# Moving three kinds of side work one place later in a fused attention and feed-forward kernel on Trainium2

## The chip, the cores and the metric

The kernel runs on one core of one Trainium2 chip. Its engines work at the same time, each through its own queue in order: TensorE (PE in the profile; PEld is its weight load), VectorE (DVE), ScalarE (ACT), GpSimd (POOL), and SyncE (SP), which issues most DMAs. They wait for each other through semaphores. The metric is the device time of one execution in microseconds (us), less is better.

## The reference

Three stages in float32, on 2304 tokens (4 batches of 576):

```python
scores = where(0 <= i - j < 64, q @ k.T / 8, -1e9)      # 8 heads of 64, causal window of 64
x = (softmax(scores) @ v)                               # laid out as [2304, 512]
x2 = ((x @ w1) * (x @ w2)) @ w3 @ w_out                 # 512 -> 1024 -> 1024 -> 512
h = x2 @ w_in                                           # 512 -> 2048
out = (h * sigmoid(h)) @ w_out2                         # 2048 -> 512
```

The weights come in as float64 and are turned into float32 on the chip.

## The kernel before

Every matrix product of float32 quality is made of three passes: an operand is split into a high part (a cast, mostly on ACT) and a low part (the difference, mostly on POOL), and high times high, high times low and low times high are summed in PSUM.

The tokens are cut into 6 blocks of 384 (`NB`). `phase_a(blk)` computes the first feed-forward stage of a block in 24 units: units 0 to 15 compute `ab` (one accumulator each; an even unit is x @ w1, copied by ACT at L582, the odd one behind it x @ w2, multiplied with it by DVE at L584 and split into `p` or `q`), units 16 to 23 compute `x2` in halves (four accumulators, copied by ACT at L561). The input of a block is `xa` and `xb`, the splits of `xr`: two of four 128-row parts, c = 0, 1, in `xa`, c = 2, 3 in `xb`. Unit 0 of a block uses c = 0, 1, 2 and then 3; for each c its three passes read high, low, high of the input.

Between the units the attention of the next block is worked in. It consists of groups (two heads, 128 queries), 12 to a block, and `half(h)` issues them in halves, two units to a group:

- an even half (even unit) issues for group g the scores (L317, L321, then DVE L327), for g - 2 the product with the values (`values`, L394 and L395), for g - 1 the transposes `t` of the normalised probabilities `sm` (L360) and their copies to `pt` (ACT L370, L372, DVE L373, L375), then the exponentials of g (ACT L338);
- an odd half issues `normalise(g)` (DVE L346, L348 and the multiply L350), the output sum of g - 2 (`total`: ACT copies L402, L403, DVE adds L404, L405, POOL add L406 into `xr`), the split of the next keys (ACT L292 `qkhi`, POOL L296 `klo`, DVE L299) and of the next values (`vhl`, ACT and POOL), and the next loads.

For the last group of a block the output sum is already issued at the end of the even half, in unit 22, ahead of the normalise in unit 23, and the last part of the next block's input (c = 3) is split right behind it, also in unit 22 (`split_x`, o == 3, f == 0). The other three parts are split in units 17, 19 and 21. Only groups from 17 on (`PLAIN`) have an output sum of this kind.

In blocks 1 to 4 the weight `w_in` is converted as well, in 16 chunks of 6 units (`Stored.pieces`): scale and rest on ACT, fraction and two halves of the sign on DVE, and with the second half of the sign the integer sum of 128x512 words on POOL (L181), in place 8 of a chunk, that is in units 2, 8, 14 and 20 of a block; the store is issued two places later. `squeeze(u)` issues the piece that is due at place u.

The last stage runs over 3 super blocks of 8 slices, `step(s, k)` with k = 0 to 6: seven products (L781) into two accumulators `hx` and `hy` in the place of eight, read by ACT and DVE between them, and the products with `w_out2` (L835). The operands of the products of the next super block are sums of parts of x2 (`x_sum`), made in the last slice: `X_AT` says at which (slice, k).

The order on each engine is the order in which this code issues the instructions (a manual schedule); only semaphores can hold an instruction back.

Of the kernel before, what the change touches and what calls it, by code (L numbers as in the profile page):

```python
# [14 lines left out]
ALU = mybir.AluOpType  # L15
# [8 lines left out]
NBLK = T // NB  # L24
NU = T // 128
NPAIR = H // 2
# [16 lines left out]
def tile_window_attention_ffn(ctx, tc, qkv, vp, mask, ident, w1, w2, w3t, w_out, w_in, w_out2, out):  # L43
# [7 lines left out]
    nc = tc.nc  # L51
# [7 lines left out]
    def f32(ap):  # L59
        return ap.bitcast(F32)  # L60
# [92 lines left out]
    class Stored(Chunk):  # L153
# [3 lines left out]
        def pieces(self):  # L157


            def scale():  # L160
                w = self.words.rearrange("p (n two) -> p n two", two=2)
                self.high = w[:, :, 1]
                self.b = slot("cv_b", "cv_b", [512], I32, bufs=CVB)
                nc.scalar.activation(out=f32(self.b), in_=f32(self.high), func=AF.Copy, scale=2.0**-112)

            def rest():
                low = self.words.rearrange("p (n two) -> p n two", two=2)[:, :, 0]
                self.r = slot("cv_r", "cv_r", [512], I32, bufs=CVR)
                nc.scalar.activation(out=self.r, in_=low.bitcast(U32), func=AF.Copy, scale=2.0**-29)

            def fraction():
                nc.vector.tensor_scalar(out=self.b, in0=self.b, scalar1=3, scalar2=None, op0=ALU.logical_shift_left)

            def sign(i):
                n = slice(i * 256, i * 256 + 256)
                nc.vector.scalar_tensor_tensor(
                    out=self.b[:, n], in0=self.high[:, n], scalar=-0x80000000, in1=self.b[:, n],
                    op0=ALU.bitwise_and, op1=ALU.bitwise_or,
                )
                if i:  # L180
                    nc.gpsimd.tensor_tensor(out=self.b, in0=self.b, in1=self.r, op=ALU.add)  # L181

            def store():
                nc.sync.dma_start(out=self.out, in_=f32(self.b))

            return [self.load, scale, rest, fraction, lambda: sign(0), lambda: sign(1), store]

    weights = {}
    line = []
    between, unit_of = {}, [0]  # L190

    def squeeze(u):
        if u in between:
            between.pop(u)()
    done = {"load": 0, "step": 0}

    def loads_to(n):
# [33 lines left out]


    NG = NU * NPAIR
    LAST_HALF = 2 * NG + 3
    qk_raw, v_raw, qk_st, v_st, s_st, p_st = {}, {}, {}, {}, {}, {}
    pt = {}

# [15 lines left out]
    def plain(g):  # L253


        return g < PLAIN
# [153 lines left out]
    def half(h):  # L410

        g, odd = divmod(h, 2)
        if not odd:
            if g < NG:
                scores(g)
            squeeze(unit_of[0])
            if 2 <= g <= NG + 1:
                sums.append(values(g - 2))  # L420
                if plain(g - 2):
                    sums.pop()()
            if 1 <= g <= NG:
                split_t(g - 1, transposes(g - 1))
            if g < NG:
                exps(g)
            if sums and (g - 2) % (3 * NPAIR) == 3 * NPAIR - 1:
                sums.pop()()
        else:
            if g < NG:  # L430
                normalise(g)
            if sums:
                sums.pop()()
            prep_qk(g + 2)
            if g < NG:
                prep_v(g)

            for x in range(g + 2, g + 5):
                if plain(x) and x > g + 2:
                    break  # L440
                load_qk(x)
            for x in range(g + 1, g + 4):
                if g < (x - 1 if plain(x - 3) else x - 3):
                    break
                load_v(x)

    halves, sums = [0], []

    def halves_to(n):
        while halves[0] < min(n, LAST_HALF):  # L450
            half(halves[0])
            halves[0] += 1

    def split_x(blk, c):
        if c == 0:
            xhl[blk] = [slot(f"{t}{blk}", t, [2, 2, NB], F32R) for t in ("xa", "xb")]
        x = xhl[blk][c // 2][:, c % 2]
        split(x[:, 0], x[:, 1], xr[:, c], "act", "pool")
# [93 lines left out]
    def phase_a(blk, hooks):  # L552
        x = xhl[blk]
        p = [slot(f"p{blk}", "p", [5, 2, NB], F32R), slot(f"q{blk}", "q", [3, 2, NB], F32R)]
        p = [p[f // 5][:, f % 5] for f in range(8)]
        a_sb = None

        def finish_x2(o, acc):
            squeeze(unit_of[0] - 1)
            x2 = slot(f"x2s{blk}_{o}", "st", [NB], bufs=4)  # L560
            nc.scalar.copy(out=x2, in_=acc)  # L561
            nc.scalar.dma_start(out=x2d[o, :, blk * NB : (blk + 1) * NB], in_=x2)

        def unit(n):
            halves_to(W_HALVES + 24 * blk + n + 1)
            hooks(n)

        for s in range(16):
            f, m = divmod(s, 2)
            unit(s)  # L570
            fs = slice((f % 4) * 128, (f % 4 + 1) * 128)
            acc = accumulator(f"ab{blk}_{s}", [128, NB])
            for k in range(4):
                w = weights["12", (2 * m + f // 4) * 4 + k]
                for n, (l, r) in enumerate(PASSES):
                    nc.tensor.matmul(  # L576
                        acc, lhsT=w[:, l, fs], rhs=x[k // 2][:, k % 2, r, :],
                        start=(k == 0 and n == 0), stop=(k == 3 and n == 2),
                    )
            if m == 0:  # L580
                a_sb = slot(f"a{blk}_{f}", "st", [2, NB], bufs=4)
                nc.scalar.copy(out=a_sb[:, 0], in_=acc)  # L582
            else:
                nc.vector.tensor_tensor(out=a_sb[:, 1], in0=acc, in1=a_sb[:, 0], op=ALU.mult)  # L584
                squeeze(unit_of[0] - 1)
                split(p[f][:, 0], p[f][:, 1], a_sb[:, 1], "act", "pool")
        kept = []
        for o in range(4):
            acc = accumulator(f"x2_{blk}_{o}", [128, NB])
            for f in range(8):  # L590
                if f % 4 == 0:
                    unit(16 + 2 * o + f // 4)
                    if blk + 1 < NBLK and o == 3 and f == 0:
                        split_x(blk + 1, 3)
                    if blk + 1 < NBLK and o < 3 and f == 4:
                        split_x(blk + 1, o)
                for n, (l, r) in enumerate(((0, 0), (1, 0), (0, 1))):
                    if o == 0 and f == 7 and n == 2:
                        continue
                    nc.tensor.matmul(  # L600
                        acc, lhsT=wp[f][:, l, o * 128 : (o + 1) * 128], rhs=p[f][:, r, :],
                        start=(f == 0 and n == 0), stop=(f == 7 and n == 2),
                    )
                if kept and f == 1:
                    first = kept.pop()
                    nc.tensor.matmul(
                        first, lhsT=wp[7][:, 0, 0:128], rhs=p[7][:, 1, :], start=False, stop=True
                    )
                    finish_x2(0, first)
            if o == 0:  # L610
                kept.append(acc)
            else:
                finish_x2(o, acc)
# [11 lines left out]
    with tc.manual_schedule():  # L625
# [5 lines left out]
        for i in range(16):  # L631
            qq, k = divmod(i, 4)
            cols = slice(qq * 512, (qq + 1) * 512)
            c = Stored(None, w_in[k * 128 : (k + 1) * 128, cols], xe[:, i % 2 * 1024 : i % 2 * 1024 + 1024], w_in32[k, :, cols])
            load, scale, rest, fraction, sign0, sign1, store = c.pieces()
            at = 6 * i
            chunks.append((load, store))
            between[at + 1], between[at + 3] = scale, rest
            between[at + 4], between[at + 6], between[at + 8] = fraction, sign0, sign1

        def drop(n):
            u = unit_of[0]
# [12 lines left out]
        for blk in range(1, NBLK - 1):  # L655
            phase_a(blk, drop)
        for u in sorted(between):
            between.pop(u)()
        chunks[15][1]()
        late.close()  # L660
        converting.update(z=lambda: ps.tile([128, 512], I32, name="cv_z", tag="ps3"), banks=3)
# [203 lines left out]
        def x_op(j, i):  # L865
            b11, b12, b21, b22 = x_sources()
            src = (b11, b11, b21, b12, b21, tmp["t1"], b22)[i]
            n = OPS * j + i
            x_tile(n)
            x_high(n, src)  # L870
            later.append(lambda: x_low(n, src))

        def x_sum(i):
# [13 lines left out]
        X_AT = {  # L887
            (5, 0): lambda j: x_raw(j), (5, 3): lambda j: x_sum(0), (6, 2): lambda j: x_sum(2),
            (6, 4): lambda j: x_op(j, 0), (6, 6): lambda j: x_sum(1), (7, 1): lambda j: x_op(j, 1),
            (7, 2): lambda j: x_op(j, 2), (7, 4): lambda j: x_sum(3), (7, 5): lambda j: x_op(j, 3),  # L890
            (8, 0): lambda j: x_op(j, 4), (8, 2): lambda j: x_op(j, 5), (8, 3): lambda j: x_op(j, 6),
        }

# [177 lines left out]
```

## Time and profile before

| what | value |
|---|---|
| median of 3 runs | 844.87 us (844.01 to 845.13) |
| the profiled execution | 844.38 us, of which the span from first to last instruction is 842.6 us |
| PE busy | 824.5 us, 98% of the span |
| DVE, ACT, POOL busy | 614.4, 560.8, 530.6 us |
| granted TensorE clock | 1.00 in the whole span |
| attention beside `phase_a`, blocks 1 to 4 | 159.6 to 412.5 us of the span |
| last block and last stage | 412.5 to 842 us |

PE busy is a sum over stages, and its matmuls are pipelined, so that small gaps between them show better in the starting times of a timeline than in the share. The chain that ended last (68% PE, 7% ACT, 6% POOL, 4% issue, 3% DVE) passes through PE for most of the span, and through ACT, DVE and POOL in parts of blocks 1 to 4.

### The profile page before, as it was taken

The page shows a single profiled execution, that of the slowest core. Times are in us where ns is not written, and L with a number is a line of the kernel's source. Part 1 is how long each engine was busy: PE and PEld are TensorE (multiplying, and loading weights), DVE is VectorE, ACT ScalarE, POOL GpSimd, SP SyncE. Part 2 cuts the span into 40 slices and gives each one's busy share as a digit, 9 for nine tenths or more (in the row PEclk, how much of TensorE's full clock was granted, in tenths as well). Part 3 has the DMA queues.
Part 4 walks back from the last instruction along what each step waited for, and adds up shares of the span by engine and source line. Part 5 has one row for each costly group of instructions (what it writes and reads, how often), then busy time and mean ns, then how long its engine had stood idle before and what let it go on. Part 6 is the DMA issues. An engine that isn't in the chain of part 4 may idle for free.

```text
span 842.6 us, 14171 instructions
## 1 busy us (share of the span) xinstructions
PE 824.5 (98%) x4410; PEld 744.9 (88%) x4410; DVE 614.4 (73%) x1420; ACT 560.8 (67%) x1389; POOL 530.6 (63%) x588
## 2 busy tenths in 40 slices
PE   5999999999999999999999999999999999999998
PEld 2555799999999999999999998888898888888986
DVE  5879877688888888888368698998644568644544
ACT  5889778898898899898556566546543446443433
POOL 5669676677677677677465577876455457454441
PEclk9999999999999999999999999999999999999999
DMA  8999334434544554543443522301301201201001
GB/s 299 315 309 289 106 96 125 145 118 142 167 157 144 170 157 145 169 152 107 134 154 114 200 75 75 125 26 51 101 25 45 106 26 63 88 25 51 1 1 75
DMA packets 57130, 102.66 MB, mean 122 GB/s; under 512 B 5472, under 2 KB 34912, under 8 KB 57056
## 3 DMA queue, kind: packets, MB, share of 16 engines
q1 hardware_dynamic: 53600, 97.05, 35.7%
q10 hardware_dynamic: 3456, 4.72, 1.5%
q8 instruction: 35, 0.57, 0.3%
q14 instruction: 39, 0.32, 0.1%
HBM read 88.11 MB, written 13.63 MB: 121 GB/s over the span
## 4 chain that ended last, share of the span: by engine, by line
PE 68%; ACT 7%; POOL 6%; issue 4%; DVE 3%; ACTq 0%; POOLq 0%; DVEq 0%
PE o L835 22%; PE ab L576 16%; PE hy L781 11%; PE hx L781 9%; PE x L600 6%; POOL klo L296 2%; ACT sm L338 1%; PE t L360 1%; POOL xr L406 1%; POOL vhl L84 1%; ACT qkhi L292 1%; PE o L394 1%; POOL p L84 1%; PE s L317 1%; POOL q L84 1%
## 5 line engine op out<-in xcount | busy, mean ns | idle before, releaser
L835 PE MATMUL o<-hl,gp 128*128 128x512 f32 x504 | 133.3, 394 | 0.0
L576 PE MATMUL ab<-xa,hl 128*128 128x384 f32 x576 | 119.0, 341 | 0.0
L781 PE MATMUL hy<-xop,j 128*128 128x384 f32 x576 | 116.0, 335 | 0.5 <-DVE tmp L675 0.5
L576 PE MATMUL ab<-xb,hl 128*128 128x384 f32 x576 | 115.4, 334 | 0.0
L84 POOL TENSOR_TENSOR gp<-tmp,gp 128x384 fp32r<-128x384 f32 x56 | 63.5, 1134 | 79.5 <-ACT gp L81 77.9
L781 PEld LDWEIGHTS hy<-xop,j 128*128 128x128 f32 x576 | 102.7, 188 | 9.8 <-DVE tmp L675 1.6
L835 PEld LDWEIGHTS o<-hl,gp 128*128 128x128 f32 x504 | 93.1, 188 | 13.1
L576 PEld LDWEIGHTS ab<-xb,hl 128*128 128x128 f32 x576 | 101.3, 188 | 0.0
L797 ACT ACTIVATE tmp<-hx 128x384 f32<-128x384 f32 x48 | 23.6, 492 | 114.0 <-DVE hx L675 69.2
L576 PEld LDWEIGHTS ab<-xa,hl 128*128 128x128 f32 x576 | 99.1, 188 | 0.0
L675 DVE TENSOR_TENSOR tmp<-hy,tmp 128x384 f32<-128x384 f32 x96 | 53.2, 554 | 56.9 <-PE hy L781 52.0
L781 PE MATMUL hx<-xop,j 128*128 128x384 f32 x432 | 86.6, 335 | 0.0
L835 PE MATMUL o<-hl,gq 128*128 128x512 f32 x324 | 85.9, 393 | 0.0
L84 POOL TENSOR_TENSOR gq<-tmp,gq 128x384 fp32r<-128x384 f32 x36 | 40.0, 1111 | 72.6 <-ACT gq L81 72.6
L781 PEld LDWEIGHTS hx<-xop,j 128*128 128x128 f32 x432 | 76.8, 188 | 4.2
L406 POOL TENSOR_TENSOR xr<-ot 128x128 f32<-128x128 f32 x55 | 32.3, 587 | 73.9 <-DVE ot L405 65.8
L296 POOL TENSOR_TENSOR klo<-qk,qkhi 64x192 fp32r<-64x192 f32 x110 | 68.0, 618 | 7.6 <-ACT qkhi L292 2.7
L835 PEld LDWEIGHTS o<-hl,gq 128*128 128x128 f32 x324 | 60.3, 188 | 11.2
L600 PE MATMUL x<-p,wp 128*128 128x384 f32 x360 | 69.6, 339 | 0.0
L338 ACT ACTIVATE sm<-sm,nm 128x192 f32<-128x192 f32 x144 | 64.5, 450 | 3.8 <-DVE nm L327 2.4
L600 PEld LDWEIGHTS x<-p,wp 128*128 128x128 f32 x360 | 61.8, 188 | 0.0
L137 POOL TENSOR_TENSOR cv_b<-cv_b,cv_r 128x512 int32<-128x512 int32 x32 | 48.6, 1520 | 18.7 <-DVE cv_b L133 9.4
(138 smaller groups left out, 1887.4 us busy)
## 6 DMA issues: line engine op xcount, KB each, us to landing
qk<-in_qkv SPq DMA_DIRECT2D x55, 384.0 KB, 3.2
words<-in_w_out SPq DMA_DIRECT2D x24, 512.0 KB, 5.4
r<-w_in SPq DMA_DIRECT2D x22, 512.0 KB, 3.4
words<-in_w3t SPq DMA_DIRECT2D x16, 512.0 KB, 6.6
words<-in_w SPq DMA_DIRECT2D x16, 512.0 KB, 6.6
xe<-in_w_in SPq DMA_DIRECT2D x16, 512.0 KB, 4.6
v<-in_qkv SPq DMA_DIRECT2D x55, 96.0 KB, 2.7
x2d<-x2s ACTq DMA_DIRECT2D x24, 192.0 KB, 1.9
```

What stands on the lines that cost most here:

```text
L84: (nc.vector if eng_lo == "dve" else nc.gpsimd).tensor_tensor(out=lo, in0=src, in1=f32(hi), op=ALU.subtract)
L137: nc.gpsimd.tensor_tensor(out=x, in0=b, in1=self.r, op=ALU.add)
L292: nc.scalar.copy(out=hi, in_=t)
L296: nc.gpsimd.tensor_tensor(out=k_lo[g % 2][hs, h * 192 : h * 192 + 192], in0=t[hs, n], in1=f32(hi[hs, n]), op=ALU.subtract)
L338: nc.scalar.activation(out=x, in_=x, func=AF.Exp, scale=-1.0, bias=nm[:, h : h + 1], accum_out=sums_of[g % 2][:, h, 0:1])
L406: nc.gpsimd.tensor_tensor(out=xr[:, c, r : r + 128], in0=t[:, 0:128], in1=t[:, 128:256], op=ALU.add)
L576: nc.tensor.matmul(acc, lhsT=w[:, l, fs], rhs=x[k // 2][:, k % 2, r, :], start=(k == 0 and n == 0), stop=(k == 3 and n == 2),)
L600: nc.tensor.matmul(acc, lhsT=wp[f][:, l, o * 128 : (o + 1) * 128], rhs=p[f][:, r, :], start=(f == 0 and n == 0), stop=(f == 7 and n == 2),)
L675: eng.tensor_tensor(out=out, in0=a, in1=b, op=op)
L781: nc.tensor.matmul(bank[name], lhsT=w[:, l, at + kt], rhs=x[:, kt, r, :], start=(fresh and kt == 0 and n == 0), stop=(kt == 1 and n == 2), ...
L797: nc.scalar.activation(out=sg, in_=src, func=AF.Sigmoid)
L835: nc.tensor.matmul(oacc[t], lhsT=g[:, l, cols], rhs=weights["out", 2 * p + i][:, r, :], start=(p == 0 and i == 0 and n == 0), stop=(p == P ...
```

## The change

Three edits:

1. The output sum of a block's last group is issued in the odd half of unit 23, behind `normalise` and so like that of every other group; the last part of the next block's input (c = 3) is split in unit 23, behind the split of the next keys and values, in place of unit 22. `LAST_HALF` grows by one so that the last group of all still gets its sum.
2. The integer sum of a `w_in` chunk on POOL becomes a piece of its own, one place later: units 3, 9, 15 and 21 of a block. Where two pieces are due at one place, both are issued, the older chunk's first.
3. In the last stage the slice sum `x_sum(3)` (DVE, 128x768) is issued at (7, 6), behind the low part of the fourth operand, instead of at (7, 4).

```diff
-                if i:
-                    nc.gpsimd.tensor_tensor(out=self.b, in0=self.b, in1=self.r, op=ALU.add)
+
+            def whole():
+                nc.gpsimd.tensor_tensor(out=self.b, in0=self.b, in1=self.r, op=ALU.add)
...
-            return [self.load, scale, rest, fraction, lambda: sign(0), lambda: sign(1), store]
+            return [self.load, scale, rest, fraction, lambda: sign(0), lambda: sign(1), whole, store]
...
     def squeeze(u):
-        if u in between:
-            between.pop(u)()
+        for f in between.pop(u, ()):
+            f()
...
-    LAST_HALF = 2 * NG + 3
+    LAST_HALF = 2 * NG + 4
...
             if g < NG:
                 exps(g)
-            if sums and (g - 2) % (3 * NPAIR) == 3 * NPAIR - 1:
-                sums.pop()()
...
                     unit(16 + 2 * o + f // 4)
-                    if blk + 1 < NBLK and o == 3 and f == 0:
-                        split_x(blk + 1, 3)
-                    if blk + 1 < NBLK and o < 3 and f == 4:
+                    if blk + 1 < NBLK and f == 4:
                         split_x(blk + 1, o)
...
-            load, scale, rest, fraction, sign0, sign1, store = c.pieces()
-            at = 6 * i
+            load, *pieces, store = c.pieces()
             chunks.append((load, store))
-            between[at + 1], between[at + 3] = scale, rest
-            between[at + 4], between[at + 6], between[at + 8] = fraction, sign0, sign1
+            for at, f in zip((1, 3, 4, 6, 8, 9), pieces):
+                between.setdefault(6 * i + at, []).append(f)
...
-            (7, 2): lambda j: x_op(j, 2), (7, 4): lambda j: x_sum(3), (7, 5): lambda j: x_op(j, 3),
+            (7, 2): lambda j: x_op(j, 2), (7, 5): lambda j: x_op(j, 3), (7, 6): lambda j: x_sum(3),
```

Where POOL goes from block 3 to block 4, its row of instructions before is this (cv_b is the integer sum of w_in, xr the add of an output sum, klo and vhl the low parts of the next keys and values, xb4 the low parts of block 4's input, first c = 2, then c = 3):

```order
L181 TENSOR_TENSOR cv_b_4338<-cv_b_4338,cv_r_4419 128x512
L406 TENSOR_TENSOR xr_88<-ot58_4623 128x128
L296 TENSOR_TENSOR klo0_75<-qk62_4479,qkhi62_4629 64x192 x2
L84 TENSOR_TENSOR vhl60_4634<-v60_4403,vhl60_4634 128x3x64
L84 TENSOR_TENSOR xb4_4484<-xr_88,xb4_4484 128x384
L406 TENSOR_TENSOR xr_88<-ot59_4686 128x128
L84 TENSOR_TENSOR xb4_4484<-xr_88,xb4_4484 128x384
L296 TENSOR_TENSOR klo1_76<-qk63_4557,qkhi63_4710 64x192 x2
L84 TENSOR_TENSOR vhl61_4715<-v61_4481,vhl61_4715 128x3x64
```

and in the changed kernel, at the same place:

```order
L407 TENSOR_TENSOR xr_88<-ot58_4622 128x128
L297 TENSOR_TENSOR klo0_75<-qk62_4479,qkhi62_4628 64x192 x2
L84 TENSOR_TENSOR vhl60_4633<-v60_4402,vhl60_4633 128x3x64
L84 TENSOR_TENSOR xb4_4484<-xr_88,xb4_4484 128x384
L182 TENSOR_TENSOR cv_b_4338<-cv_b_4338,cv_r_4419 128x512
L407 TENSOR_TENSOR xr_88<-ot59_4702 128x128
L297 TENSOR_TENSOR klo1_76<-qk63_4557,qkhi63_4708 64x192 x2
L84 TENSOR_TENSOR vhl61_4713<-v61_4481,vhl61_4713 128x3x64
L84 TENSOR_TENSOR xb4_4484<-xr_88,xb4_4484 128x384
```

The integer sum went from ahead of the first four rows to behind them, and the low part of c = 3 from ahead of klo and vhl to behind them.

At the same place on DVE (rs and sm are the normalise of group 61, ot59 the output sum of the block's last group) the row is, before:

```order
L375 TENSOR_TENSOR pt0_975<-t60_4674,pt0_975 64x64 x2
L404 TENSOR_TENSOR ot59_4686<-o59_4670,ot59_4686 64x256
L405 TENSOR_TENSOR ot59_4686<-o59_4670,ot59_4686 64x256
L346 TENSOR_REDUCE rs61_4666<-es1_83 128x2
L348 RECIPROCAL rs61_4666<-rs61_4666 128x2
L350 TENSOR_TENSOR sm1_74<-sm1_74,rs61_4666 128x384
```

and in the changed kernel:

```order
L376 TENSOR_TENSOR pt0_975<-t60_4674,pt0_975 64x64 x2
L347 TENSOR_REDUCE rs61_4666<-es1_83 128x2
L349 RECIPROCAL rs61_4666<-rs61_4666 128x2
L351 TENSOR_TENSOR sm1_74<-sm1_74,rs61_4666 128x384
L405 TENSOR_TENSOR ot59_4702<-o59_4670,ot59_4702 64x256
L406 TENSOR_TENSOR ot59_4702<-o59_4670,ot59_4702 64x256
```

The two adds of the output sum changed places with the normalise. TensorE's own order is the same in both kernels.

## Rows read from the trace of the kernel before

**Rows 1.** Waits of TensorE: engine, line, releaser: us in total, times, longest us

```profile
PE t L360 <- ACT xb L81: 1.3, 5, 0.3
PE hy L781 <- DVE tmp L675: 0.5, 1, 0.5
```

**Rows 2.** Stages: us, busy PE, PEld, DVE, ACT, POOL, PE clock, DMA share, GB/s

```profile
287.40:351.40 64.00, 63.52 (x400) 63.10 (x398) 54.82 (x176) 56.41 (x165) 46.81 (x65) 1.00 0.51 157
...
412.50:475.00 62.50, 62.50 (x359) 61.97 (x358) 41.88 (x53) 35.65 (x68) 38.37 (x34) 1.00 0.48 163
```

**Rows 3.** Timeline, TensorE, blocks 3 to 4: start us, us, engine, line, instruction

```profile
344.92 0.28 PE L395 MATMUL o<-pt,vhl 128*128 128x256 f32 x1
345.41 0.52 PE L360 MATMUL t<-id_sb,sm 128*128 128x128 f32 x3 [0.22 <-ACT xb L81]
...
351.11 0.52 PE L360 MATMUL t<-id_sb,sm 128*128 128x128 f32 x3 [0.26 <-ACT xb L81]
...
352.53 1.20 PE L576 MATMUL ab<-xb,hl 128*128 128x384 f32 x6
...
356.28 0.28 PE L395 MATMUL o<-pt,vhl 128*128 128x256 f32 x1
356.40 0.49 PE L360 MATMUL t<-id_sb,sm 128*128 128x128 f32 x3
```

**Rows 4.** Timeline, VectorE: the normalise multiplies of units 17, 21 and 23

```profile
333.63 0.56 DVE L350 TENSOR_TENSOR sm<-sm,rs 128x384 f32<-128x384 f32 x1
...
343.61 1.65 DVE L350 TENSOR_TENSOR sm<-sm,rs 128x384 f32<-128x384 f32 x1
...
350.41 0.56 DVE L350 TENSOR_TENSOR sm<-sm,rs 128x384 f32<-128x384 f32 x1
```

**Rows 5.** Timeline, GpSimd: units 17, 18 and the end of block 3

```profile
335.15 0.58 POOL L406 TENSOR_TENSOR xr<-ot 128x128 f32<-128x128 f32 x1 [1.44 <-DVE ot L405]
...
337.67 1.01 POOL L84 TENSOR_TENSOR xa<-xr,xa 128x384 fp32r<-128x384 f32 x1
...
343.56 1.29 POOL L181 TENSOR_TENSOR cv_b<-cv_b,cv_r 128x512 int32<-128x512 int32 x1
...
351.15 1.01 POOL L84 TENSOR_TENSOR xb<-xr,xb 128x384 fp32r<-128x384 f32 x1 [0.62 <-ACT xb L81]
352.12 1.46 POOL L296 TENSOR_TENSOR klo<-qk,qkhi 64x192 fp32r<-64x192 f32 x2
```

**Rows 6.** Timeline, ScalarE: ends of exponentials in units 16 and 22, and block 4's beginning

```profile
333.02 0.18 ACT L338 ACTIVATION_READ_ACCUMULATOR sm<-sm,nm 128x1 f32 x1
...
348.20 0.19 ACT L338 ACTIVATION_READ_ACCUMULATOR sm<-sm,nm 128x1 f32 x1
...
350.56 0.51 ACT L81 CAST xb<-xr 128x384 fp32r<-128x384 f32 x1 [1.53 <-POOL xr L406]
...
354.57 0.48 ACT L582 COPY a<-ab 128x384 f32<-128x384 f32 x1
```

**Rows 7.** Timeline, ScalarE and TensorE, from block 0 to block 1

```profile
156.23 0.19 ACT L338 ACTIVATION_READ_ACCUMULATOR sm<-sm,nm 128x1 f32 x1
...
160.82 1.20 PE L576 MATMUL ab<-xb,hl 128*128 128x384 f32 x6
```

**Rows 8.** Timeline, VectorE, then TensorE, slices 7 and 8 of the last stage

```profile
577.17 0.94 DVE L675 TENSOR_TENSOR xe<-xe,xra 128x768 f32<-128x768 f32 x1
...
578.51 0.54 DVE L675 TENSOR_TENSOR tmp<-hy,tmp 128x384 f32<-128x384 f32 x1
...
583.99 0.56 DVE L675 TENSOR_TENSOR tmp<-hy,tmp 128x384 f32<-128x384 f32 x1 [0.42 <-PE hy L781]
...
577.07 1.55 PE L835 MATMUL o<-hl,gp 128*128 128x512 f32 x6
579.11 1.31 PE L781 MATMUL hy<-xop,j 128*128 128x384 f32 x6 [0.48 <-DVE tmp L675]
...
587.55 1.21 PE L781 MATMUL hy<-xop,j 128*128 128x384 f32 x6
```

More of the change, by code (lines that the diff above doesn't have):

```diff
@@ L657, in tile_window_attention_ffn @@
         for u in sorted(between):
-            between.pop(u)()
+            squeeze(u)
         chunks[15][1]()
```

## The prediction

> **What bounds the kernel now.** I read the waits of TensorE first [rows 1]: in the attention stage its transposes `t` wait five times, 1.3 us together, and in the last stage one product `hy` waits 0.48. Then the stages [rows 2]: block 3 has 63.52 us of TensorE work in 64.00, and after the attention, from 412.5 on, 62.50 in 62.50. So TensorE sets the pace, nothing behind block 4 can take up a delay, and what it gains or loses between units 16 and 1 of a block stays in the time unless it is given back inside blocks 1 to 4.
>
> The waits are larger than the view lists. Normally `t` starts 0.12 us after the second product with the values (356.28, 356.40); at 345.41 it starts 0.49 after it, 0.37 late, of which 0.22 is flagged [rows 3]. Adding that 0.15 to each of the five, they cost 1.3 + 5 x 0.15 = 2.05 us. They stand at unit 0 of blocks 2, 3 and 4 and at unit 22 of blocks 2 and 3. (Some smaller, unflagged ones I leave out.) The profile names ACT xb as the releaser, but `t` needs the normalise: in both cases in [rows 3] `t` starts 0.14 to 0.15 after the end of L350 (343.61 + 1.65 = 345.26; 350.41 + 0.56 = 350.97) [rows 4].
>
> At unit 22 the reason is a collision. L350 took 1.65 us in place of 0.56: the integer sum on POOL had begun at 343.56, 0.05 ahead of it, ended at 344.85, and L350 ended 0.41 later [rows 4, 5]. The Trainium skill (SBUF — State Buffer, Who interferes with whom) says that a VectorE instruction with two SBUF inputs and a GpSimd instruction that reads SBUF contend for a shared pair of ports, that whoever issues first has it for the whole instruction, and that issue order decides who blocks. This pair of rows agrees. At unit 0 the reason is the order: normalise stands behind the adds of the output sum.
>
> **Edit 2, the integer sum.** It removes the 0.37 at unit 22. At its new place in unit 21 it follows the low part of c = 2 on POOL; what that does to unit 23 is under edit 1. In units 3, 9 and 15 it goes ahead of the low part of `p` or `q`, so that the next normalise meets an instruction of 1.29 us instead of one of 1.01 [rows 5]: at most 0.3 each, and at unit 17, where slack is least, in three blocks 0.9 in all. I take 0, since TensorE, made late by edit 1, has the slack; 0.9 goes into the range. The integer sum itself has no reader near; the store that waits for it on SP stands one place later still, with loads behind it that are not due for a unit.
>
> **Edit 1, the output sum and c = 3.** Step by step from block 3 to block 4.
> - The exponentials of unit 22 end at 348.39 [rows 6]. In unit 17 the multiply starts 0.43 after them (333.20, 333.63) [rows 4, 6], so in unit 23 it is ready at 348.82, not at 350.41.
> - POOL: in unit 17 the add `xr` starts 1.52 after that multiply starts (335.15) and the low part behind `klo` and `vhl` ends 3.53 after that (338.68) [rows 5]. In unit 21, with its multiply no longer held, `xr` starts at 345.13, the low part of c = 2 ends at 348.66, and the integer sum follows at once, to 349.9. It is ahead of the multiply by some 0.2 us. So the collision moves with it: L350 ends at 349.9 + 0.41 = 350.3, and `t` can go at 350.45.
> - TensorE, without the 0.37 and its own 0.41 (0.26 + 0.15), would be at `t` at 351.11 - 0.78 = 350.33. This wait is practically gone.
> - But the input c = 3 is now last. Adds and `xr` follow L350's end by 0.96 (334.19 to 335.15): `xr` at 351.3. Then POOL does `klo`, `vhl` and only then the low part: 3.53 later, 354.85. Before it stood ahead of `klo` and ended at 351.15 + 1.01 = 352.16 [rows 5].
> - TensorE needs this low part in unit 0: of the six matmuls at 352.53 [rows 3] the first three are c = 2, the fifth reads the low part of c = 3, some 0.7 in: 353.2. Before, the margin was 1.0 us. After, it comes there at 353.2 - 0.8 = 352.4, or up to 0.4 later where it has been late against ScalarE; I take 352.6. **A new wait of 354.85 - 352.6 = 2.2 us.** Bounds: 1.65 if TensorE has gained nothing by then (353.2), 2.5 if it has all of it.
>
> Does it come back? ScalarE's copy of unit 0 starts at 354.57 [rows 6]; with the last two matmuls of the accumulator ending near 355.4 it slides by 0.8. ScalarE works in order, and all that the next boundary rests on (`pt`, exponentials, output sums, casts) is behind that copy. So TensorE and the side work slide together, and the next boundary pays again. The gain on ScalarE, which stood 1.53 us at 350.56 waiting for `xr` [rows 6], isn't one either: with `xr` now ending near 351.9, that cast waits longer, behind `qkhi` and `vhl`.
>
> Three boundaries (to blocks 2, 3, 4) pay 2.2 each: 6.6. From block 0 to 1 there is no `w_in` work yet, so no collision: exponentials end at 156.42 [rows 7], multiply 156.85 to 157.41, `xr` 158.37, low part 161.9; TensorE needs it at 160.82 + 0.7 = 161.5 [rows 7]: 0.4 us. From block 4 to 5 no normalise is left and POOL holds no `klo` and `vhl`: 0.
>
> **Edit 3, the slice sum.** The product `hy` at 579.11 waited for the DVE add of 578.51 to 579.05, behind the slice sum of 0.94 us at 577.17 [rows 8]. Without it the add ends near 578.15, before TensorE wants to start: the flagged 0.48 and the 0.15 that is not flagged are saved, 0.65. At the new place the sum delays the add of 583.99 by 0.94, or by 1.7 if POOL is reading then; it would end by 586.3, and the next `hy` product starts at 587.55 [rows 8]: cost 0. The same sum one super block later makes no wait before, and saves none.
>
> **Sum:** -2.05 - 0.65 + 0.4 + 6.6 = +4.3 us on the profiled execution's 844.38: 848.7. That run lies 0.49 below the median of 844.87; the small waits left out, about as large in sum, pull the other way, so I leave it at **848.7 us**.
>
> **Rivals.**
> 1. *Normalise first.* The multiply is issued before the integer sum in unit 23; the margin is 0.2 us on times pieced together from unit 17. Then L350 runs 348.82 to 349.38, the integer sum after it to about 350.7, still ahead of `xr` in POOL's queue; `xr` at 350.7 instead of 351.3, the low part 0.6 to 0.7 earlier, three times: 848.7 - 2.1 = 846.6. The skill's rule on issue order, named above, leads to this if DVE is first and to the forecast if POOL is.
> 2. *The low part is in time (not slower).* If POOL finished it by 352.6, 2.2 us before my time, the gains stand alone: 844.38 - 2.7 = 841.7. For it: 1.0 us of margin before, and a normalise ready 1.6 earlier. Against it: `klo` and `vhl` ahead of it in POOL's order, 3.53 from `xr` to its end. Halfway, if each boundary cost only what the first does: 844.38 - 2.7 + 4 x 0.4 = 843.3.
> 3. *Clock.* After a wait of 2 us the granted clock falls from 2.4 to 1.2 GHz and the next two units' 4.2 us take twice as long: three times 4.2 more, 861. Against it: 1.00 in both stages of [rows 2] with their waits, though none of those is as long.
>
> **Chances.** Forecast 0.70, rival 1 0.13, rival 2 0.05 and its halfway case 0.07, rival 3 0.02, other slower ends 0.03. A measurement of this kernel can tell about 0.2%, 1.7 us: 843.2 to 846.6 counts as no change. Slower: 0.70, half of rival 1, rival 3, the rest: 0.81. Same: half of rival 1 and most of the halfway case: 0.13. Faster: 0.06. The range takes in rival 1 with a little more (845.8) and, above, waits of 2.5 each and the 0.9 of edit 2 (850.5).
>
> **What would show it.** Right: a wait of TensorE at L575 for POOL `xb` at unit 0 of blocks 1 to 4, about 0.4 and then three near 2.2; the low part of c = 3 behind `vhl`; L351 of unit 23 some 1.5 us long; no flagged wait of `t` at unit 22; no wait of `hy` near slice 7's end. The forecast is wrong if that L575 wait is missing or under 1 us, or if blocks 2 to 4 make it up before unit 16 of the next one.

## The result and the profile after

The changed kernel takes 850.42 us (median of 6 runs, 849.47 to 853.02), the kernel before 845.08 beside it: 1.0072 of its time, interval 1.0061 to 1.0083. On the 844.87 of the forecast that is 851.0, slower as predicted, but 2.3 us above the 848.7 and 0.5 above the range's upper end of 850.5. (The 850.42 as it stands lies just inside, but the kernel before beside it was 0.2 us slower than the forecast's base.) The profiled execution took 849.7 with a span of 847.8 us, 5.2 more than that of before.

First the waits of TensorE (engine, line, releaser: total us, times, longest). The lines of [rows 1] are gone from the attention of blocks 1 to 4 and from the last stage, and one is new:

```profile
PE ab L575 <- POOL xb L84: 6.0, 4, 1.9
```

The timeline from block 3 to block 4, the place of [rows 3 to 6] (start us, us, engine, line, instruction). TensorE:

```profile
354.70 0.28 PE L396 MATMUL o<-pt,vhl 128*128 128x256 f32 x1
354.82 0.49 PE L361 MATMUL t<-id_sb,sm 128*128 128x128 f32 x3
355.06 1.29 PE L575 MATMUL ab<-xa,hl 128*128 128x384 f32 x6
356.20 0.98 PE L575 MATMUL ab<-xb,hl 128*128 128x384 f32 x4
359.11 0.62 PE L575 MATMUL ab<-xb,hl 128*128 128x384 f32 x2 [1.93 <-POOL xb L84]
359.56 1.20 PE L575 MATMUL ab<-xa,hl 128*128 128x384 f32 x6
...
362.39 0.49 PE L361 MATMUL t<-id_sb,sm 128*128 128x128 f32 x3
```

`t` at 354.82 stands 0.12 behind the product with the values: no wait is left there. Four matmuls later TensorE stops. The group of four starts at 356.20 and a matmul takes 0.173 (six start within 1.04: 359.56 to 360.60), so the next two could have gone at 356.89 and went at 359.11: 2.22 us, of which 1.93 is flagged. Counted so, the four waits are 0.38, 2.19, 2.21 and 2.22 (block 1's is flagged with 0.21).

Why it waits is seen on VectorE (first line), GpSimd and ScalarE (last two):

```profile
353.08 1.51 DVE L351 TENSOR_TENSOR sm<-sm,rs 128x384 f32<-128x384 f32 x1
...
351.91 1.01 POOL L84 TENSOR_TENSOR xb<-xr,xb 128x384 fp32r<-128x384 f32 x1
352.88 1.29 POOL L182 TENSOR_TENSOR cv_b<-cv_b,cv_r 128x512 int32<-128x512 int32 x1
355.56 0.58 POOL L407 TENSOR_TENSOR xr<-ot 128x128 f32<-128x128 f32 x1 [1.38 <-DVE ot L406]
356.10 1.33 POOL L297 TENSOR_TENSOR klo<-qk,qkhi 64x192 fp32r<-64x192 f32 x2
357.50 0.59 POOL L84 TENSOR_TENSOR vhl<-v,vhl 128x192 fp32r<-128x192 f32 x1
358.05 1.00 POOL L84 TENSOR_TENSOR xb<-xr,xb 128x384 fp32r<-128x384 f32 x1
...
356.17 0.52 ACT L81 CAST xb<-xr 128x384 fp32r<-128x384 f32 x1 [1.76 <-POOL xr L407]
...
359.76 0.48 ACT L581 COPY a<-ab 128x384 f32<-128x384 f32 x1 [0.59 <-PE ab L575]
```

The integer sum begins 0.20 ahead of the multiply and the multiply takes 1.51 in place of 0.56, ending 0.42 after it. Everything behind is late: `xr`, `klo`, `vhl` and last the low part of c = 3, to 359.05. ScalarE's copy of unit 0 then waits for TensorE, so the side work slides with it.

That is the mechanism of the forecast. What it lacks is here, two boundaries earlier (from block 1 to block 2): TensorE behind a wait of the same length, and then the windows (us, busy time of PE, PEld, DVE, ACT, POOL, granted clock, DMA share, GB/s) of this place and of the two later boundaries:

```profile
222.54 0.49 PE L361 MATMUL t<-id_sb,sm 128*128 128x128 f32 x3
...
226.80 0.61 PE L575 MATMUL ab<-xb,hl 128*128 128x384 f32 x2 [1.91 <-POOL xb L84]
227.25 1.64 PE L575 MATMUL ab<-xa,hl 128*128 128x384 f32 x6
228.68 2.12 PE L575 MATMUL ab<-xb,hl 128*128 128x384 f32 x6
...
231.67 0.49 PE L361 MATMUL t<-id_sb,sm 128*128 128x128 f32 x3
```

```profile
227.00:228.00 1.00, 1.00 (x6) 1.00 (x6) 0.80 (x3) 0.54 (x2) 0.00 (x0) 0.93 0.81 303
228.00:229.00 1.00, 1.00 (x4) 1.00 (x4) 0.21 (x1) 0.96 (x3) 0.00 (x0) 0.50 0.14 45
229.00:231.00 2.00, 2.00 (x9) 2.00 (x8) 1.14 (x4) 1.37 (x3) 1.20 (x3) 0.50 0.00 0
231.00:232.00 1.00, 1.00 (x9) 1.00 (x8) 0.88 (x4) 0.52 (x1) 0.92 (x2) 0.87 0.00 0
...
294.00:296.00 2.00, 2.00 (x13) 2.00 (x13) 0.99 (x3) 1.56 (x4) 0.00 (x0) 1.00 0.49 180
...
360.00:362.00 2.00, 2.00 (x14) 2.00 (x13) 1.04 (x4) 1.95 (x5) 0.00 (x0) 1.00 0.21 65
```

Here the granted clock was 0.50 from 228 to 231, that is 1.2 instead of 2.4 GHz, and six matmuls of 128x384 took up to 2.12 us in place of 1.20. Behind the two later waits, as long as this one, it stayed at 1.00. From `t` of unit 0 to `t` of unit 2 this boundary took 9.13 us (222.54 to 231.67), and the same stretch at 359.11 took 7.57 (354.82 to 362.39): the fall cost 1.56.

The last stage, the place of [rows 8], VectorE and then TensorE:

```profile
583.67 0.55 DVE L671 TENSOR_TENSOR tmp<-hy,tmp 128x384 f32<-128x384 f32 x1
...
587.36 1.77 DVE L671 TENSOR_TENSOR xe<-xe,xra 128x768 f32<-128x768 f32 x1
...
582.96 1.55 PE L831 MATMUL o<-hl,gp 128*128 128x512 f32 x6
584.35 1.23 PE L777 MATMUL hy<-xop,j 128*128 128x384 f32 x6
...
587.85 1.21 PE L777 MATMUL hy<-xop,j 128*128 128x384 f32 x6
```

The product that waited 0.48 follows at once (584.35), and the slice sum at its new place takes 1.77 and makes nobody wait.

### The profile page after: what moved, and what is told of

It reads as the page before. It is cut to its first block, busy times and chain, and to the rows that moved or that the text cites. A ratio compares the mean times of both kernels' runs of the same rounds, so it can differ in the third digit from the quotient of the medians.

```text
span 847.8 us, 14176 instructions
## 1 busy us (share of the span) xinstructions
PE 825.1 (97%) x4410; PEld 746.1 (88%) x4410; DVE 614.5 (72%) x1420; ACT 562.1 (66%) x1389; POOL 529.3 (62%) x588
## 4 chain that ended last, share of the span: by engine, by line
PE 77%; POOL 4%; ACT 3%; issue 2%; DMA 1%; DVE 1%; ACTq 0%; POOLq 0%; DVEq 0%
PE o L831 24%; PE ab L575 22%; PE hy L777 12%; PE hx L777 9%; PE x L597 6%; PE t L361 2%; DMA xe<-in_w_in 1%; POOL klo L297 1%; PE o L395 1%; PE s L318 1%; PE s L322 1%; POOL xb L84 1%; POOL vhl L84 1%; PE o L396 1%; ACT sm L339 1%
## 5 line engine op out<-in xcount | busy, mean ns | idle before, releaser
L575 PE MATMUL ab<-xb,hl 128*128 128x384 f32 x576 | 117.7, 338 | 6.0 <-POOL xb L84 6.0
```

The lines of the kernel that those rows point to most:

```text
L575: nc.tensor.matmul(acc, lhsT=w[:, l, fs], rhs=x[k // 2][:, k % 2, r, :], start=(k == 0 and n == 0), stop=(k == 3 and n == 2),)
```

## The experiments

Times are medians; each ratio, with its 95% interval, is to the kernel before measured beside it. "By starts" means: the time that a matmul started later than it would have behind the one ahead of it, as counted above. "Late `t`" means: the start of `t` less that of the product with the values ahead of it, less the usual 0.12. Counted so over the attention of blocks 1 to 4, the kernel before loses 2.43 us and the changed kernel none.

**Each edit alone.** Edit 1:

```diff
-    LAST_HALF = 2 * NG + 3
+    LAST_HALF = 2 * NG + 4
...
-            if sums and (g - 2) % (3 * NPAIR) == 3 * NPAIR - 1:
-                sums.pop()()
...
-                    if blk + 1 < NBLK and o == 3 and f == 0:
-                        split_x(blk + 1, 3)
-                    if blk + 1 < NBLK and o < 3 and f == 4:
+                    if blk + 1 < NBLK and f == 4:
                         split_x(blk + 1, o)
```

> Edit 1 alone (output sum behind the normalise, c = 3 split behind keys and values); the integer sum and the slice sum stay where they were. Theory (the low part of c = 3 is late on GpSimd): the integer sum again holds the multiply of unit 21, so the low part of c = 2 ends at 349.75 of the old time scale and holds the multiply of unit 23 instead; the low part of c = 3 ends only 0.15 us earlier than in the changed kernel. Waits of TensorE for POOL xb at unit 0: about 0.2 flagged at block 1 and 1.7 to 1.9 at blocks 2 to 4; hy still waits 0.48. Time 849 to 851 us, as slow as all three edits, less if the clock does not fall, and the granted clock dips behind some of the long waits. Rival (the integer sum at its new place makes the wait): no wait over 1 us, 844 to 846 us.

Measured: 846.7 us, 1.0031 (1.0018 to 1.0044), clock 1.00. The multiply, the low part of c = 2 beside it, and the wait at the last boundary:

```profile
350.02 0.94 DVE L350 TENSOR_TENSOR sm<-sm,rs 128x384 f32<-128x384 f32 x1
...
349.53 1.01 POOL L84 TENSOR_TENSOR xb<-xr,xb 128x384 fp32r<-128x384 f32 x1
...
355.48 0.62 PE L574 MATMUL ab<-xb,hl 128*128 128x384 f32 x2 [1.46 <-POOL xb L84]
```

The wait is there without edit 2, but shorter: by starts 0.37, 1.67, 1.65 and 1.63, because the multiply takes 0.94 and not 1.51: it meets the low part of c = 2, which ends at 350.54, and not the integer sum. No `t` is late. Sum: 5.3 of waits less 2.43 gives +2.9; measured +2.3. I had expected more, 849 to 851: the integer sum's new place is needed for waits of 2.2 us, and no fall of the clock came behind the shorter ones.

Edit 2, its two main places (the whole stands in the change above):

```diff
...
-                if i:
-                    nc.gpsimd.tensor_tensor(out=self.b, in0=self.b, in1=self.r, op=ALU.add)
+            def whole():
+                nc.gpsimd.tensor_tensor(out=self.b, in0=self.b, in1=self.r, op=ALU.add)
...
+            for at, f in zip((1, 3, 4, 6, 8, 9), pieces):
+                between.setdefault(6 * i + at, []).append(f)
```

> Edit 2 alone (integer sum one place later). Theory: the waits of t at unit 22 (0.37 us) go, those at unit 0 stay and take over what is saved, since the last output sum on the way to them is not earlier; no wait for POOL xb; clock 1.000; 844.3 to 845.3 us, no difference that can be measured. Rival (edit 2 by its collisions with the normalise in units 5, 11, 17 makes the loss): 847 us or more, with waits of t in those units.

Measured: 845.19 us, 1.001 (1.0001 to 1.002). Unit 22's late `t` is gone, but late `t` in all rises from 2.43 to 3.33: 0.33 now at unit 18, and 0.3 more at each unit 0. TensorE, VectorE and GpSimd at unit 18 of block 3:

```profile
334.24 0.28 PE L396 MATMUL o<-pt,vhl 128*128 128x256 f32 x1
334.69 0.52 PE L361 MATMUL t<-id_sb,sm 128*128 128x128 f32 x3 [0.18 <-DVE sm L351]
...
333.77 0.77 DVE L351 TENSOR_TENSOR sm<-sm,rs 128x384 f32<-128x384 f32 x1
...
332.85 1.29 POOL L182 TENSOR_TENSOR cv_b<-cv_b,cv_r 128x512 int32<-128x512 int32 x1
```

The integer sum now meets the multiply of unit 17, which took 0.56 in [rows 4]. Alone, edit 2 is a loss of 0.8 us, at the edge of what the interval tells, and the trace has 0.9 of it.

Edit 3, and edits 2 and 3 together:

```diff
-            (7, 2): lambda j: x_op(j, 2), (7, 4): lambda j: x_sum(3), (7, 5): lambda j: x_op(j, 3),
+            (7, 2): lambda j: x_op(j, 2), (7, 5): lambda j: x_op(j, 3), (7, 6): lambda j: x_sum(3),
```

> Edit 3 alone (slice sum two places later). Theory: the wait of hy for DVE tmp (0.48 flagged, 0.65 by starting times) goes and nothing takes its place: 844.2 us, 0.6 to 0.7 less than before, at the edge of what three rounds can tell; the trace shows it. Rival (the sum at its new place delays the operands of slice 8): a new wait of 0.3 us or more in slice 8, no gain.

> All but edit 1. Theory (edit 1 is the whole loss): 843.8 to 844.8 us, clock 1.000, no wait for POOL xb. Rival (the edits make the loss only together): 847 us or more.

Measured: edit 3 takes 843.48 us, 0.9992 (0.9983 to 1.0002), the wait of `hy` gone and no new one; both take 844.76, 1.0006 (0.9996 to 1.0015), without any wait for `xb`. So the loss needs edit 1. The single edits add up to 2.3 + 0.8 - 0.9 = 2.2 us, while the change costs 5.3: edits 1 and 2 together cost more than each alone, by the collision that makes the waits 2.2 and by the clock.

**Edit 1 in halves.** Only the split of c = 3 goes later, the output sum stays in unit 22 (the other edits are undone):

```diff
-                    if blk + 1 < NBLK and o == 3 and f == 0:
-                        split_x(blk + 1, 3)
-                    if blk + 1 < NBLK and o < 3 and f == 4:
+                    if blk + 1 < NBLK and f == 4:
                         split_x(blk + 1, o)
```

> Half of edit 1: only the split of c = 3 is issued a unit later (behind keys and values); the output sum stays ahead of the normalise, the other two edits are left out. Theory (the lateness is made of two parts: the normalise with its collision ahead of xr, and klo and vhl ahead of the low part): xr stays at its old time, ScalarE no longer stands 1.5 us, the low part ends about 1.3 us later than before at 353.4 of the old time scale against a need at 353.2: waits for POOL xb under 0.4 flagged, clock 1.000, 843.5 to 845.5 us. Rival (the place of c = 3 alone makes the whole wait): waits of 1.5 or more at three boundaries, 846.5 us or more.

Measured: 846.66 us, 1.0028 (1.0017 to 1.0039). At the last boundary:

```profile
351.46 0.52 PE L360 MATMUL t<-id_sb,sm 128*128 128x128 f32 x3 [0.36 <-ACT xb L81]
...
354.39 0.62 PE L576 MATMUL ab<-xb,hl 128*128 128x384 f32 x2 [0.66 <-POOL xb L84]
```

My expectation was too low, and the rival's waits of 1.5 did not come either. Standing behind `klo` and `vhl` costs by itself (0.83 by starts, at each of three boundaries), and `t` of unit 0 is late as well (0.52 each, 1.57 in all). By the medians this half alone costs as much as all of edit 1, whose other half, normalise first, makes the wait longer but frees `t`. The profiled execution was the fastest of seven (845.54), and its waits and late `t` add up to 2.0 more than those of before, so that part of the median's 2.5 is not shown by the trace.

**The order on GpSimd.** Edits 1 and 3, with the low part of c = 3 issued ahead of `klo` and `vhl`, once with the integer sum at its old place and once with edit 2:

```diff
+    def boundary(g):
...
+            nc.scalar.copy(out=hi, in_=t)
...
+            nc.scalar.copy(out=vhl[:, :, 0], in_=v)
+        split_x(blk, 3)
...
+                nc.gpsimd.tensor_tensor(
+                    out=k_lo[g % 2][hs, h * 192 : h * 192 + 192], in0=t[hs, n], in1=f32(hi[hs, n]), op=ALU.subtract
+                )
...
+            nc.gpsimd.tensor_tensor(out=vhl[:, :, 1], in0=v, in1=f32(vhl[:, :, 0]), op=ALU.subtract)
```

> Edits 1 and 3, but at the block boundary GpSimd makes the low part of c = 3 ahead of klo and vhl (ScalarE keeps the order keys, values, c = 3). The integer sum stays at its old place. Theory: the low part ends 1.3 us earlier than with edit 1 alone, whose wait was 1.65 by starting times: 0.3 to 0.4 is left at blocks 2 to 4, none at block 1, clock 1.000, no wait of hy; 843 to 844.5 us, as fast as edit 3 alone or up to 0.5 faster. Rival (TensorE would wait for the keys or values instead, which are now last): new waits at L318 to L322 or L395 of unit 2, 845 us or more.

> All three edits, with the low part of c = 3 ahead of klo and vhl on GpSimd as in the run before. Theory: the wait of 2.2 by starting times shrinks by 1.3 to 0.9, at block 1 to none; no wait is long enough for the clock to fall, 1.000 in all runs; 844 to 846 us. Rival (the clock falls because of where the integer sum is, not of the wait): clock below 1.000 and 847 us or more.

Measured: 843.04 us, 0.9987 (0.9978 to 0.9997), and with edit 2 844.82, 1.001 (1.0001 to 1.002). Neither trace has a wait for keys or values. The loss of the change is gone in the first and down to 0.7 us in the second, so edit 2 costs 1.8 us here, against 0.8 alone. The second also answers the rival on the clock: the integer sum is at its new place, the waits are 0.90 by starts as expected, and the clock is 0.999 or 1.00 in all ten runs. So the place of the integer sum by itself does not lower the clock. Whether the first beats edit 3 alone was measured again, the two beside each other:

> Edits 1 and 3, with the integer sum at its old place, and GpSimd makes the low part of c = 3 ahead of klo and vhl at the block's end. It repeats the run that came out at 0.9987 of the kernel before. If the edit itself is worth something beyond edit 3, it lies below edit 3 alone in this call: 842.7 to 843.4 against 843.5. If its gain is edit 3's alone, the two are equal within 0.3.

> Edit 3 alone again, beside the run above, on the same chip: 0.9992 of the kernel before as it was, 0.65 us less by the wait that it removes.

Measured: 843.69 us, 0.9993 (0.9984 to 1.0001), and 843.62, 0.9995 (0.9986 to 1.0004): equal. GpSimd and TensorE of the former at the last boundary:

```profile
351.58 0.58 POOL L406 TENSOR_TENSOR xr<-ot 128x128 f32<-128x128 f32 x1 [1.38 <-DVE ot L405]
352.78 1.00 POOL L84 TENSOR_TENSOR xb<-xr,xb 128x384 fp32r<-128x384 f32 x1 [0.62 <-ACT xb L81]
353.74 1.25 POOL L424 TENSOR_TENSOR klo<-qk,qkhi 64x192 fp32r<-64x192 f32 x2
...
353.84 0.62 PE L600 MATMUL ab<-xb,hl 128*128 128x384 f32 x2 [0.46 <-POOL xb L84]
```

Even first in the row the low part waits for `xr` and ScalarE's cast, and TensorE for it: 0.46 flagged where `t` was 0.41 late before. The wait has changed its place, and what is left is edit 3's gain. No version was found that is faster than the kernel before by more than can be measured.

**More work ahead of c = 3 on TensorE.** The changed kernel, but unit 0 of blocks 1 to 4 takes c = 0, 1, 2 of units 0 and 1 first:

```diff
...
+            if blk and s == 0:
+                part(0, (0, 1, 2))
+                part(1, (0, 1, 2))
+                part(0, (3,))
+            elif blk and s == 1:
+                part(1, (3,))
...
```

(`part(s, ks)` does the products of unit s with the parts ks, in the same passes as before.)

> All three edits, with GpSimd's order as in the changed kernel; only TensorE's order in units 0 and 1 of a block is changed: c = 0, 1, 2 of both units first, then c = 3 of both. It works 9 matmuls (1.56 us) more before it needs the low part of c = 3. Theory: the wait of 2.2 by starting times shrinks to about 0.65, block 1 has none, clock 1.000 in all runs; the side work still slides by the copy of unit 0, so the gain is 1.6 once and the feedback of 0.3 to 0.4 a block: 845 to 846.5 us against 848 of the changed kernel without falls of the clock. Rival (the wait is not for the low part of c = 3): no change, 849 us or more.

Measured: 848.5 us, 1.0052 (1.0035 to 1.0069), clock 1.00 in every run. A smaller gain than expected. The waits of TensorE for `xb`, and `t` in unit 18 of block 3:

```profile
PE ab L577 <- POOL xb L84: 1.7, 3, 0.6
```

```profile
336.44 0.28 PE L396 MATMUL o<-pt,vhl 128*128 128x256 f32 x1
336.94 0.52 PE L361 MATMUL t<-id_sb,sm 128*128 128x128 f32 x3 [0.21 <-DVE sm L351]
```

By starts the waits fall from 7.00 to 2.2 (0.73 each) and the clock's 1.56 is saved, but late `t` is back, 4.07 us in 21 places where the changed kernel has none: 7.00 - 2.2 + 1.56 - 4.07 leaves 2.3, as much as the spans of the two profiled executions differ (847.8 and 845.5); the medians differ by 1.9. A TensorE that is held up less at the boundary catches up with the normalise, as in the row above, where L351 releases `t`; there the next limit stands.

**The clock.** The changed kernel with `klo` written twice at the end of a block, so that the low part of c = 3 comes later still; and the changed kernel itself again:

```diff
-        for h, hs in HEADS:
+        twice = (g - 2) % (3 * NPAIR) == 1 and g > 26
+        for h, hs in HEADS * 2 if twice else HEADS:
             n = slice(384 + h * 192, 576 + h * 192)
             nc.gpsimd.tensor_tensor(
```

> The kernel after, but GpSimd writes the low half of the keys (klo) twice at the end of a block, so the low part of c = 3 comes some 1.3 us later at four boundaries. Without any fall of the clock the kernel after takes about 848.0 (its 849.7 with one fall of 1.56). Theory 1, the clock falls when a wait at the boundary is long enough, and 2.2 us is only just that: the three later waits grow to about 3.5 us, each of them is followed by a fall in every execution, and block 1's wait of .4 becomes 1.7; 848.0 + 4 x 1.3 + 3 x 1.55 = 857.9, clock .993 to .995. Rival, that the falls come by chance at these places whatever the length: one to three falls as in the kernel after, 854.8 to 857.9, with executions apart by multiples of 1.5. Rival, that the wait isn't the cause: clock .997 to .998 as after, and the waits alone, 854 to 855.

> The changed kernel itself, beside the others of this call. Theory: its executions lie on steps of about 1.5 us by the number of falls of the clock behind the three long waits: 848.0 with none (clock 1.000), 849.6 with one (.998), 851.1 with two (.997), 852.8 with three (.995). Rival, that its executions scatter without steps or that the clock has nothing to do with the spread: times between 849 and 853 whose clock shows no order.

Measured, the longer wait: 858.18 us (857.45 to 858.43), 1.0163 (1.0149 to 1.0177), clock 0.993 or 0.994 in each of four runs. TensorE at its last boundary, and windows behind the three long waits:

```profile
365.22 0.62 PE L576 MATMUL ab<-xb,hl 128*128 128x384 f32 x2 [3.24 <-POOL xb L84]
365.68 1.64 PE L576 MATMUL ab<-xa,hl 128*128 128x384 f32 x6
367.12 2.12 PE L576 MATMUL ab<-xb,hl 128*128 128x384 f32 x6
```

```profile
230.00:232.00 2.00, 2.00 (x8) 2.00 (x8) 1.20 (x3) 1.96 (x5) 0.31 (x1) 0.50 0.03 10
...
298.00:300.00 2.00, 2.00 (x8) 2.00 (x7) 1.01 (x3) 1.95 (x6) 0.09 (x1) 0.50 0.08 21
...
367.00:369.00 2.00, 2.00 (x8) 2.00 (x7) 1.20 (x3) 1.77 (x4) 0.84 (x2) 0.50 0.00 0
```

Now the clock falls behind all three waits. From `t` of unit 0 to `t` of unit 2 the last of them took 10.46 us (359.63 to 370.09), against 7.57 in the changed kernel: 1.31 of longer wait and 1.58 of clock. This is close to the 857.9 that was expected if each of the longer waits is followed by a fall. The first rival, chance whatever the length, is not far off on time (its upper end is the same), but it doesn't say why all three fall, with a mean clock as low in all four runs; the second, that the wait isn't the cause, is out.

Measured, the changed kernel again: 849.7 us (848.92 to 851.84), 1.0068 (1.0054 to 1.0083). Of its profiled execution the windows behind the three waits:

```profile
228.00:232.00 4.00, 4.00 (x19) 4.00 (x17) 2.24 (x7) 2.86 (x6) 2.12 (x4) 0.58 0.02 6
...
295.00:299.00 4.00, 4.00 (x28) 4.00 (x27) 3.20 (x10) 3.68 (x10) 2.15 (x4) 1.00 0.04 10
...
361.00:365.00 4.00, 4.00 (x27) 4.00 (x27) 3.71 (x12) 3.69 (x12) 2.80 (x5) 1.00 0.05 11
```

Again one fall of three, behind the same wait. The clean steps that I expected do not show: 848.92 came with a mean clock of 0.997, 849.65 and 849.76 with 0.997 and 0.998, 851.84 with 0.995. Only the slowest run of each set has the lowest clock (853.02 of the first also has 0.995). But in none of the ten runs of the changed kernel is the mean clock above 0.998, and in edit 1 alone and the reordered kernel, with waits up to 1.5 us flagged, none is below 0.999. So a fall goes with the waits of 1.9 us, and by the mean clocks there are more of them in some runs than in others; in which places they fell is known of the two profiled executions only.

## Why the prediction was right in its mechanism and missed the time

- **TensorE sets the pace** [rows 2]: right. Waits, late `t` and the clock account for the span: -2.43 of late `t`, -0.75 in the last stage, +7.00 at the four boundaries, +1.56 of clock give +5.4, against 5.2.
- **Late `t`, -2.05:** right in kind, 0.4 too small for the small ones left out. That the normalise and not ScalarE's cast releases `t` held too: with normalise moved ahead, every late `t` disappeared, although that cast (356.17) now starts after `t` (354.82).
- **Edit 2 at 0:** the term holds in the changed kernel, where no `t` is late at unit 18, and the bound of 0.9 is what it costs at unit 18 when it is alone (1.09 late there against 0.20); what it adds at units 0 (0.9) and saves at units 22 (0.9) cancels. Its real price lies in the step that the forecast counted under edit 1, the collision in unit 23. Edit 1 without it waits 1.65 us a boundary instead of 2.2 and does not lose the clock.
- **The collision goes to unit 23, GpSimd first by 0.2 us:** right. The integer sum led by 0.20, and the multiply ended 0.42 after it. The sentence of the Trainium skill (SBUF — State Buffer, Who interferes with whom) that issue order decides agrees once more, and rival 1, normalise first, did not happen.
- **The new wait of 2.2 us three times and 0.4 once:** right (2.19, 2.21, 2.22 and 0.38), and it slid on as foreseen. Block after block nothing was given back. That it came out to within 0.03 is luck in part: the forecast had 0.4 of choice in when TensorE comes there (352.4 to 352.8), and bounds of 1.65 and 2.5.
- **Edit 3, -0.65:** right. From `t` of unit 2 behind the last boundary to the end it was 486.19 us before and 485.37 after; without a late `t` of 0.07 that is 0.75 less, and the slice sum took 1.77, the upper of its two values, at no cost.
- **The clock: here the forecast failed.** It priced each new wait at its own length and put the fall of the clock behind it at nothing: that fall was rival 3, given 0.02 on the ground that no wait of before lowers the clock, "though none of those is as long". That showed nothing on a wait of 2.2 us, and the forecast made three of them. The rival also had the form wrong: each wait followed by two units at half speed, 4.2 us more each. In fact the low clock held for some 3 us in which six matmuls took up to 0.92 us more, 1.56 a time, behind one of the three waits in each of the two profiled executions. The 848.7 is, within 0.6, the changed kernel without a fall (849.7 - 1.56 = 848.1); one more term of 1.56 gives 850.3, against 851.0 measured on that base. The profiled execution was one of the faster ones (mean clock 0.998; 0.995 in the slowest), so that the rest fits more falls in other runs, which no trace shows. A rival of "one to three falls at 1 to 2 us" should have carried a real chance and moved the upper end to about 853.

The Trainium skill (TensorE: Matmul & The Clock Gate, HAM oscillation — how this bites in real kernels) describes a kernel whose TensorE waits for data at each tile and so starts every next tile at the low clock. The longer wait agrees in that all three were followed by a fall, though some 1 us after TensorE had resumed; of the change's own three waits one was.

Open: why of three equal waits it is the first that was followed by a fall in both profiled executions. As the three are equal, the length of the wait alone doesn't decide it. No run varied what TensorE did ahead of the wait at a constant length.

## What to carry to other kernels

Before a late producer is moved behind other work on an in-order engine, list everything that then stands ahead of it and price its consumer's wait: here 1.3 us of `klo`, 0.6 of `vhl` and a collision's 0.95 stood against a margin of 1.0 us, and the wait was 2.2 at each block. When a forecast itself contains a new TensorE wait longer than any in its stage, price the clock as well, from what matmuls cost at either level, since the clock of before says nothing on it. A freed wait is worth only what the next limit leaves: the cure that took the loss away gained nothing beyond edit 3.

## What the runs showed of the hardware that was not expected

- The granted clock fell not during the wait but after it: TensorE resumed at 226.80, and the windows show 0.93 from 227 to 228 and 0.50 from 228 to 231, while it was busy all the time.
- From about 15 us on, waits of up to 1.7 us (flagged; the longest of these is for `sm` at 32.79 in the changed kernel) left the clock at 1.00; of those of 1.9 us some were followed by a fall; of those of 3.2 us all three of the profiled execution were. The price was the same behind both, 1.56 and 1.58 us. (The 1.00 in the whole span of the kernel before does not fit its first 14 us, where TensorE waits 6.98 us for its first input: four matmuls of 128x512 took 3.78 us from 9.83 on, eight took 3.74 from 14.81 on.)
- An engine's flagged wait was 0.15 to 0.3 us shorter than the time that its starts lost (1.93 against 2.22), as for the `t` of [rows 3].
